# mLSTM cell and multiplicative FFN on one core: input rows loaded once, ScalarE copies, and y through DRAM as whole rows

## The chip, the core and the metric

The kernel runs on one core of one Trainium2 chip. Such a core has TensorE (PE in the profile; its weight loads are listed apart as PEld), VectorE (DVE), ScalarE (ACT), GpSimd (POOL) and SyncE (SP), which issues most of the DMAs. Each engine works through its own instructions in program order; engines wait for each other only through semaphores. A DMA that an engine issues waits in that engine's queue of instructions like any other instruction, and what stands behind it waits too.

The metric is the device time of one execution in microseconds (us), lower is better.

## The reference, cut to what matters

```python
# mLSTM cell; q, k, v, o_gate: (4, 8, 768, 40), gates: (4, 8, 768)
for t in range(S):
    m_new = np.maximum(f_gate[:, :, t] + m, i_gate[:, :, t])
    f_stab = np.exp(f_gate[:, :, t] + m - m_new)
    i_stab = np.exp(i_gate[:, :, t] - m_new)
    C = f_stab * C + i_stab * np.einsum('bhd,bhe->bhde', vt, kt)
    n = f_stab * n + i_stab * kt
    h_tilde = np.einsum('bhde,bhe->bhd', C, qt)
    denom = np.maximum(np.abs(np.einsum('bhd,bhd->bh', n, qt)), 1.0)
    y[:, :, t] = sigmoid(o_gate[:, :, t]) * h_tilde / denom
# FFN on x = y as (3072, 320)
out = ((x @ w1) * (x @ w2)) @ w3 @ w_out        # 320 -> 1024 -> 1024 -> 320
```

## The kernel before, in words

**Units and steps.** The sequence is cut into 24 units: unit n is 128 tokens of one batch entry (`c, b = divmod(n, 4)`) with all 8 heads. The main loop (L820) runs over 32 steps s. Step s computes the scores and the state update of unit s and the outputs of unit s-1, and around them the FFN of earlier units. PE's instructions are chained in program order by `in_order` (L84). The other engines follow the order in which the loop emits their instructions.

**Inside a step** (`quarter_work`, L338). PE multiplies the masked weights with v (`ph`, L363: the own outputs, from the unit's own tokens), the queries with the state (`pi`, L366), keys with queries (`ss`, L389) and keys with weighted values (`pc`, L394). `ph` and `pi` lie in the PSUM tile cell[1], `ss` and `pc` in cell[0]. DVE then makes the outputs of unit s-1 (`outputs`, L419): h = pi x gate (L423), plus `ph` in four quarters of 64x164 (L430), then the denominator from the 41st column of h, which is the normalizer's product because v carries a column of ones (L534): absolute value (L438), maximum with 1 and times 2 (L440), reciprocal (L441), (tanh+1) x reciprocal into the gate's tile (L443), times h into y (L445). Between these stand the masked scores (L397) and the two state additions (L404, L414); POOL multiplies the state by its decay (L335) between the two additions.

**Weights of a unit.** ACT makes the exponentials (L303, eight instructions), POOL cuts the triangle out of them (`masks`, L308) and weights v (L330).

**Turned queries and keys.** Up to unit 9 PE transposes k and q and ACT copies them out (`turn`, L320 to L325). From unit 10 on the loads `load_turned` (L141) bring rows of four tokens (160 elements), and two DVE transposes of 32x32 blocks (L317) give kT and qT. One head of 40 elements needs two blocks, of 32 and of 8 columns, so every row is loaded twice, the second time into 32 other partitions and 32 columns further left: 8 DMAs of 80 KB for a unit. `load_turned(s + 2)` is emitted at the end of step s (L975), into one of two buffers (halves of `gates` and `q_all`).

**From y to the FFN.** The FFN wants x with channels in partitions. Up to unit 14 (NY = 15, L126) PE transposes y in three 128x128 blocks (`x_trans`, L478) and ACT copies them out (L486). These run at the start of step n+3, at L849. POOL first copies the last 64 columns of y once more (`twice`, L475), for a pair of 64-row matmuls. From unit 15 on y goes to DRAM and back: `send(s - 2)` at the start of step s writes 32-column pieces by four DMAs (L451), `get_back(s - 2)` reads them by four DMAs into the one buffer `yb` (L462), and `x_turn(s - 2)` transposes them on DVE after the step's outputs (L926).

**FFN.** Units are taken in groups of four. Groups 0 to 2 go through `up` (L618): 24 blocks, of which steps 14 and 15 do the last four, for units 10 and 11. Groups 3 to 5 go through `up_by_seven` (L668), which forms products by a seven-product scheme. It needs sums of the weights, made by POOL in steps 16 and 17 (`weight_sums`, L651, eight additions of 128x512), and sums of the tokens of a group, made by DVE (`token_sums`, L661), for group 3 in step 17, behind the turned y of unit 15 and kT and qT of unit 18. In steps 19 to 24 its first products (p15) go into cell[1], from where ACT copies them out (L702, L704), and then the output matmuls of earlier groups (`ffn_out`, L733) write to the same banks of cell[1]. Before that, in steps 16 to 18, PE has little FFN work other than `ffn_out`.

**SP's queue** in a step, in order: send (from step 17), U rows (L159), k, v and o_gate of unit s+2 (L139, L153), get_back, at the step's end load_turned, and the weights still to come (L184, up to step 12).

Of the kernel before, what the change touches and what calls it, by code (L numbers as in the profile page):

```python
# [8 lines left out]
FP = mybir.dt.float32  # L9
U32 = mybir.dt.uint32  # L10
AF = mybir.ActivationFunctionType
OP = mybir.AluOpType
# [4 lines left out]
def kernel(  # L17
# [41 lines left out]
    KF = DM // P  # L59
    REM = DM - KF * P  # L60
# [7 lines left out]
    sb = ctx.enter_context(tc.tile_pool(name="sb", bufs=2))  # L68
    dram = ctx.enter_context(tc.tile_pool(name="dram", bufs=1, space=bass.MemoryType.DRAM))
# [39 lines left out]

    NB, NBQ, NBV = 4, 3, 5  # L110
    N_DVE = N_U = 10
    N_DIAG = 2
# [4 lines left out]
    vbuf = [v_all[:, i * H * D1:(i + 1) * H * D1].rearrange("p (h d) -> p h d", d=D1) for i in range(NBV)]  # L117
# [5 lines left out]
    decay = const.tile([P, B * NP, NT], FP, name="decay")  # L123
    UT = const.tile([P, 2, 3, BH], FP, name="UT")
    U_d = dram.tile([NT, BH, L], FP, name="U_d")
    NY = 15  # L126
    KC = KF + 1
    y_d = [dram.tile([P, 4, KC, 32], FP, name=f"y_d{n}") if n >= NY else None for n in range(NU)]

    o_t, u_t = {}, {}  # L130

# [9 lines left out]
    def load_turned(n):  # L141
        c, b = divmod(n, B)
        for dst, src in zip(turned_in[n % 2], (k, q)):
            for hip in range(2):
                of = src[b].rearrange("(p two) s d -> two p s d", two=2)[hip, :, c * P:(c + 1) * P, :]
                for j in range(2):
                    p0, c0 = hip * DP + j * 32, (1 - j) * 32
                    nc.sync.dma_start(out=dst[p0:p0 + 32, c0:c0 + NP * RAW].rearrange("r (p e) -> r p e", p=NP),  # L148
                                      in_=of.rearrange("p (r f) d -> r p (f d)", f=4))

    def load_o(n):
        o_t[n] = io.tile([P, H, D], FP, name="o_in", tag="o_in", bufs=5)
# [80 lines left out]
    def scale_next(early=False):  # L233
        scaled.append(pend.pop(0))
        scale(scaled[-1][1], early)
# [31 lines left out]
    qT_t, kT_t, vw_t, before_t, y_t, x_t = {}, {}, {}, {}, {}, {}  # L267
# [43 lines left out]
    def turn(n):  # L311


        if n >= N_DVE:
            for src, dst, name in zip(turned_in[n % 2], (kT_t, qT_t), ("kT", "qT")):
                dst[n] = sb.tile([128, NP, P], FP, name=name, tag=name)
                done = nc.vector.transpose(out=dst[n].rearrange("i p (r f) -> i p f r", f=4),  # L317
                                           in_=src[:, 32:TB].rearrange("i (p f d) -> i p f d", p=NP, f=4)[:, :, :, 0:32])
# [100 lines left out]
    def outputs(n, pi, ph):  # L419
        c, b = divmod(n, B)  # L420
        hs = slice(b * H, (b + 1) * H)
        h = sb.tile([P, H, D1], FP, name="h", tag="h")
        nc.vector.tensor_tensor(out=h.rearrange("p (n two) d -> p two n d", two=2), in0=pi,  # L423
                                in1=gT[:, c, hs].rearrange("p (n two) -> p two n", two=2).unsqueeze(3)
                                .to_broadcast([P, 2, NP, D1]), op=OP.mult)
        if n < N_DIAG:
            nc.vector.tensor_tensor(out=h, in0=ph, in1=h, op=OP.add)
        for x, e in quarters if n >= N_DIAG else ():
            part = h[halves[x], 0:H // 2] if x == e else h[halves[x], H // 2:H]
            nc.vector.tensor_tensor(out=part, in0=ph[x][halves[e]], in1=part, op=OP.add)  # L430

        den = sb.tile([P, H, 1], FP, name="den", tag="den")

        def steps():
            V = nc.vector
            yield V.tensor_scalar(out=den.bitcast(U32), in0=h[:, :, D:D1].bitcast(U32), scalar1=0x7FFFFFFF, scalar2=None,  # L438
                            op0=OP.bitwise_and)
            yield V.tensor_scalar(out=den, in0=den, scalar1=1.0, scalar2=2.0, op0=OP.max, op1=OP.mult)  # L440
            yield V.reciprocal(out=den, in_=den)  # L441
            e = o_t.pop(n)
            nc.vector.scalar_tensor_tensor(out=e, in0=e, scalar=1.0, in1=den.to_broadcast([P, H, D]), op0=OP.add, op1=OP.mult)  # L443
            y_t[n] = sb.tile([P, DM + REM], FP, name="y", tag="y")
            yield nc.vector.tensor_tensor(out=y_t[n][:, 0:DM].rearrange("p (h d) -> p h d", d=D), in0=h[:, :, 0:D],  # L445
                                           in1=e, op=OP.mult)

        done = steps()
        return lambda: next(done)

    def send(n):  # L451


        y = y_t.pop(n)
        for cc in range(KF):
            nc.sync.dma_start(out=y_d[n][:, :, cc, :], in_=y[:, cc * P:(cc + 1) * P].rearrange("t (i c) -> t i c", c=32))
        for i in range(0, 4, 2):
            nc.sync.dma_start(out=y_d[n][:, i:i + 2, KF, :], in_=y[:, KF * P:DM].rearrange("t (i c) -> t i c", c=32))

    back_t = {}  # L460

    def get_back(n):  # L462
        back_t[n] = sb.tile([P, 4, KC, 32], FP, name="yb", tag="yb", bufs=1)
        for i in range(4):
            nc.sync.dma_start(out=back_t[n][32 * i:32 * (i + 1)].rearrange("r m k c -> r m (k c)"),
                              in_=y_d[n][:, i].rearrange("(m r) k c -> r m (k c)", r=32))

    def x_turn(n):
        gr, j = divmod(n, GT)
        if j == 0:  # L470
            x_t[gr] = ffn.tile([128, KC, TG], FP, name="xT", tag="xT")
        nc.vector.transpose(out=x_t[gr][:, :, j * P:(j + 1) * P].rearrange("c k (m r) -> c k m r", r=32),
                            in_=back_t.pop(n).rearrange("r m k c -> r k m c"))

    def twice(n):  # L475
        nc.gpsimd.tensor_copy(out=y_t[n][:, DM:DM + REM], in_=y_t[n][:, KF * P:DM])
# [13 lines left out]
    TC = GC * L  # L490
    RG = GR * BH
    RAW = 4 * D
    TB = 32 + NP * RAW
    gates = const.tile([P, 2 * TB], FP, name="gates")
    f_sb, a, F, U, on = (gates[0:RG, i * TC:(i + 1) * TC] for i in range(5))

    turned_in = [[mem[:, i * TB:(i + 1) * TB] for i in range(2)] for mem in (gates, q_all)]
    w, g = f_sb, on
# [32 lines left out]
        if i < NBQ:  # L531
            nc.gpsimd.memset(qbuf[i][:, :, D:DP], 0.0)
    for i in range(NBV):
        nc.gpsimd.memset(vbuf[i][:, :, D:D1], 1.0)  # L534
    for t in state:
        nc.gpsimd.memset(t[0], 0.0)
    nc.gpsimd.memset(gates[:, 5 * TC:2 * TB], 0.0)
    nc.gpsimd.memset(gates[RG:P, NP * RAW:TB], 0.0)
# [279 lines left out]
    turned, converted, fetched = 0, 2, 5  # L818

    for s in range(len(n_up)):  # L820
        if NY <= s - 2 < NU:
            send(s - 2)
        if N_U <= s + 3 < NU:
            load_u(s + 3)
        if s < 3:
# [16 lines left out]
        if s < NU:  # L842
            if s >= B:
                decayed(state[s % B][1], state[s % B][0], s, 0)
        if s == 2 or N_DVE < s < NY + 2:
            twice(s - 2)
        if NY <= s - 2 < NU:
            get_back(s - 2)
        while s >= N_DVE and turned < min(s - 2, NY):  # L849
# [68 lines left out]
        with tc.issue_after(gated.ins) if gated else nullcontext():  # L918
            if seven:
                seven[3]()  # L920
            for _ in range({NU: 1, NU + 1: 3}.get(s, 0)):
                next(wsums)
            if s == NU + 1:
                ab_sums(*summed.pop(0))
            if NY <= s - 2 < NU:
                x_turn(s - 2)  # L926
            for n in () if s == 1 else (s + 2,) if s < B else (s + 2, s + 3) if s == B else (s + 3,):
                if n < N_U:
                    rows_of_u(n)
            if N_DVE <= s + 1 < NU:  # L930
                gated = turn(s + 1)
            if s - 2 in range(4 * GT - 1, NU, GT):
                token_sums((s - 2) // GT)
            if s < len(n_up) - 2 and n_out[s + 1] and s > NU + 2:
                ab_sums(*summed.pop(0))
# [76 lines left out]
```

## Time and profile before

| | |
|---|---|
| runs, us | 424.92, 426.45, 426.75; median 426.45 |
| span of the profiled execution, first to last instruction | 425.8 us |
| time of the profiled execution beyond its span | not listed; the median of the runs is 0.65 us above the span |
| busy in the span, PE / PEld / DVE / ACT / POOL | 414.1 / 335.3 / 313.5 / 150.1 / 154.3 us |
| mean granted TensorE clock | 0.996 |
| DMA | 51.15 MB, 120 GB/s in the mean |

The busy time of an engine is the time in which it shows an instruction at work. The chain of waits follows the work back from the last instruction. The timeline lists the instructions of each engine with start, duration and, in square brackets, how long the engine stood idle before it and what ended that. In this document "step 16" means s = 16, and times are us from the start of the span.

### The profile page before, as it was taken

How to read it: one execution, taken by the hardware profiler on the slowest of the kernel's cores; microseconds unless marked ns; L12 is line 12 of the kernel's file. 1: busy time of each engine (PE TensorE's matmuls, PEld its weight loads, DVE VectorE, ACT ScalarE, POOL GpSimd, SP SyncE). 2: the span in 40 equal slices, each digit the busy share in tenths (PEclk: the TensorE clock that was granted, in tenths of full speed). 3: DMA queues.
4: the chain of work that ended last, by engine and by line, in shares of the span. 5: the costliest groups of instructions: out<-in, count | busy, mean ns of one | idle time of the engine just before them, and what ended most of it. 6: DMA issues, size and time to landing. Idle time of an engine off the chain costs nothing.

```text
span 425.8 us, 13079 instructions
## 1 busy us (share of the span) xinstructions
PE 414.1 (97%) x5353; PEld 335.3 (79%) x5353; DVE 313.5 (74%) x635; ACT 150.1 (35%) x404; POOL 154.3 (36%) x211
## 2 busy tenths in 40 slices
PE   7989989999999999999999999999999999999996
PEld 4768878888688788787777778788778879888896
DVE  6676986888949779778736966596868699575971
ACT  4766865567723623630433313032311110210000
POOL 4421342233303303303307751546453587542100
PEclk9989999999999999999999999999999999999999
DMA  8999998598977776985425675756421120000001
GB/s 186 204 173 245 214 144 140 134 193 180 215 183 154 166 182 135 181 164 105 89 80 130 153 141 121 142 133 117 87 44 36 35 39 2 31 2 31 2 32 62
DMA packets 135211, 51.15 MB, mean 120 GB/s; under 512 B 109360, under 2 KB 126960, under 8 KB 135152
## 3 DMA queue, kind: packets, MB, share of 16 engines
q1 hardware_dynamic: 131552, 46.29, 53.9%
q10 hardware_dynamic: 3600, 4.03, 2.7%
q8 instruction: 42, 0.69, 0.7%
q14 instruction: 17, 0.14, 0.1%
HBM read 44.50 MB, written 5.80 MB: 118 GB/s over the span
## 4 chain that ended last, share of the span: by engine, by line
PE 53%; issue 20%; DVE 7%; POOL 7%; SPq 7%; DMA 5%; ACT 1%; POOLq 0%; DVEq 0%
PE cell L92 17%; PE pa L92 12%; PE o L92 8%; PE pb L92 8%; PE p L92 3%; POOL pw L308 3%; SPq L184 3%; DVE w3T L666 2%; PE pt L95 1%; POOL vw L330 1%; SPq L148 1%; DMA raw<-in_moe_w_dram 1%; PE fill L92 1%; POOL raw L659 1%; POOL state L335 1%
## 5 line engine op out<-in xcount | busy, mean ns | idle before, releaser
L335 POOL TENSOR_TENSOR state<-state,decay 128x164 f32<-128x164 f32 x40 | 20.0, 500 | 154.8 <-DVE state L404 129.0
L92 PE MATMUL pa<-xT,w 128*128 128x256 f32 x240 | 60.4, 382 | 0.0
L92 PEld LDWEIGHTS pa<-xT,w 128*128 128x128 f32 x240 | 44.4, 190 | 6.8 <-DVE h L430 0.4
L303 ACT ACTIVATE pw<-pw,aT 128x64 f32<-128x64 f32 x184 | 46.4, 339 | 3.2 <-ACT o_sb L741 1.9
L92 PE MATMUL pb<-xT,w 128*128 128x256 f32 x192 | 45.4, 379 | 0.0
L729 POOL TENSOR_TENSOR ab<-ab,a_sb 128x512 f32<-128x512 f32 x22 | 29.4, 1356 | 32.2 <-DVE ab L684 32.2
L92 PEld LDWEIGHTS pb<-xT,w 128*128 128x128 f32 x192 | 36.4, 190 | 5.0
L711 POOL TENSOR_TENSOR wo<-wo 128x512 f32<-128x512 f32 x22 | 27.4, 1268 | 29.8 <-DVE wo L686 29.8
L92 PE MATMUL pa<-xT,wr 64*64 64x256 f32 x384 | 37.0, 386 | 0.5 <-DVE wr L200 0.5
L92 PE MATMUL wp<-wo,w3T 128*128 128x320 f32 x128 | 35.9, 433 | 1.1 <-DVE ab L639 0.6
L308 POOL TENSOR_SCALAR_AFFINE_SELECT pw<-pw 64x512 f32<-64x512 f32 x48 | 35.8, 746 | 3.0 <-ACT pw L303 1.2
L92 PE MATMUL pb<-xT,wr 64*64 64x256 f32 x384 | 36.4, 380 | 0.0
L92 PE MATMUL cell<-w3o,ab 128*128 128x320 f32 x128 | 35.4, 432 | 0.0
L638 ACT ACTIVATE a_sb<-pa 128x512 f32<-128x512 f32 x24 | 14.3, 598 | 59.0 <-PE pb L92 59.0
L639 DVE TENSOR_TENSOR ab<-pb,a_sb 128x512 f32<-128x512 f32 x24 | 16.4, 688 | 23.2 <-ACT a_sb L638 22.8
L92 PEld LDWEIGHTS wp<-wo,w3T 128*128 128x128 f32 x128 | 23.8, 190 | 10.5 <-DVE ab L639 0.8
L92 PEld LDWEIGHTS cell<-w3o,ab 128*128 128x128 f32 x128 | 24.3, 190 | 9.5
L92 PEld LDWEIGHTS pa<-xT,wr 64*64 64x64 f32 x384 | 18.9, 132 | 15.4 <-issue 8.8
L686 DVE SCALAR_TENSOR_TENSOR a_sb<-pa,wo 128x512 f32<-128x512 f32 x12 | 8.3, 689 | 29.8 <-PE pa L92 29.8
L430 DVE TENSOR_TENSOR h<-cell,h 64x164 f32<-64x164 f32 x88 | 28.6, 326 | 1.6
L92 PE MATMUL po<-w3o,ab 128*128 128x320 f32 x96 | 26.4, 433 | 0.0
L92 PEld LDWEIGHTS po<-w3o,ab 128*128 128x128 f32 x96 | 18.1, 190 | 7.3
(180 smaller groups left out, 846.4 us busy)
## 6 DMA issues: line engine op xcount, KB each, us to landing
raw<-in_moe_w_dram SPq DMA_DIRECT2D x64, 128.0 KB, 3.4
kbuf<-in_k_dram SPq DMA_DIRECT2D x24, 160.0 KB, 4.5
v_all<-in_v_dram SPq DMA_DIRECT2D x24, 160.0 KB, 4.9
o_in<-in_o_gate_dram SPq DMA_DIRECT2D x24, 160.0 KB, 4.8
pw<-U_d SPq DMA_DIRECT2D x28, 128.0 KB, 3.5
raw<-in_moe_w_dram SPq DMA_DIRECT2D x5, 512.0 KB, 6.7
raw<-in_moe_w_out_dram SPq DMA_DIRECT2D x8, 320.0 KB, 4.1
gates<-in_k_dram SPq DMA_DIRECT2D x28, 80.0 KB, 2.5
```

What stands on the lines that cost most here:

```text
L92: in_order(nc.tensor.matmul(out, lhsT=lhsT, rhs=rhs, start=start, stop=stop))
L184: nc.sync.dma_start(out=dst, in_=src)
L303: nc.scalar.activation(out=pw[:, h, :], in_=src[:, h, :], func=AF.Exp, bias=aT[:, c, b * H + h:b * H + h + 1])
L308: nc.gpsimd.affine_select(out=pw[r], in_=pw[r], compare_op=OP.is_ge, fill=0.0, base=0, pattern=[[0, H], [1, L]], channel_multiplier=-1)
L335: nc.gpsimd.tensor_tensor(out=new, in0=old, op=OP.mult, in1=decay[:, b * NP:(b + 1) * NP, 2 * c + x:2 * c + x + 1] .to_broadcast([P, NP, D1]))
L430: nc.vector.tensor_tensor(out=part, in0=ph[x][halves[e]], in1=part, op=OP.add)
L638: nc.scalar.mul(out=a_sb, in_=pa, mul=UP ** -2)
L639: nc.vector.tensor_tensor(out=ab_t[gr][j][:, fs[0]:fs[-1] + 1, t0:t0 + a_sb.shape[-1]], in0=pb, in1=a_sb, op=OP.mult)
L666: nc.vector.tensor_tensor(out=dst, in0=p, in1=q, op=OP.subtract)
L686: nc.vector.scalar_tensor_tensor(out=out, in0=p, scalar=UP ** -2, in1=q, op0=OP.mult, op1=OP.add)
L711: aside_by.tensor_tensor(out=kept[j][:, 1:4:2], in0=kept[j][:, 1:3], in1=kept[j][:, 3:4].to_broadcast([128, 2, TH]), op=OP.add)
L729: aside_by.tensor_tensor(out=t[:, f:FO:FH, :], in0=t[:, f:FO:FH, :], in1=a, op=OP.mult)
```

## The change

- `load_turned` loads every row of four tokens once (4 DMAs of 80 KB in place of 8). A new function `shift` lets ACT copy the last 8 columns of each token into the 32 other partitions: four copies of 32x(16x8) for a unit, emitted in step n-1 ahead of the exponentials. POOL clears 32 partitions of `gates` for it in step 4.
- NY goes from 15 to 10: y of units 10 to 14 goes through DRAM too, and their PE transposes and ACT copies go away. `y_d` holds whole rows of 384 columns, written by one DMA and read by four of 384 pieces of 32 columns. So POOL's `twice` now runs for all units. `twice(s - 1)` and `send(s - 1)` stand at the end of step s, ahead of `load_turned`; `get_back` stays.
- From unit 10 (N_OWN) ACT copies the four quarters of `ph` out of PSUM into h, DVE writes pi x gate into the tile that later holds y, and adds both by one instruction of 128x328.
- The column of ones holds 2. The denominator is min(|1/x|, 0.5): reciprocal, one small instruction for the absolute value, the minimum and the product with h, and (tanh+1) times that: four instructions in place of five.

In the two programs' instruction lists, POOL's `twice` of units 15 and 16 stands behind the four additions of `weight_sums` of steps 16 and 17. ACT's `shift` stands behind the copies of `ph` and ahead of the exponentials. The first of the four copies of `ph` waits for DVE.

```diff
-                for j in range(2):
-                    p0, c0 = hip * DP + j * 32, (1 - j) * 32
-                    nc.sync.dma_start(out=dst[p0:p0 + 32, c0:c0 + NP * RAW]...)
+                nc.sync.dma_start(out=dst[hip * DP:hip * DP + 32, 32:TB].rearrange("r (p e) -> r p e", p=NP),
+                                  in_=of.rearrange("p (r f) d -> r p (f d)", f=4))
+    def shift(n):
+        for mem in turned_in[n % 2]:
+            e = mem[:, 32:TB].rearrange("r (g d) -> r g d", d=D)
+            for p0 in (0, DP):
+                nc.scalar.copy(out=e[p0 + 32:p0 + 64, :, 0:D - 32], in_=e[p0:p0 + 32, :, 32:D])
...
-    NY = 15
+    NY = 10
-    y_d = [dram.tile([P, 4, KC, 32], FP, ...) if n >= NY else None for n in range(NU)]
+    y_d = [dram.tile([P, KC * P], FP, ...) if n >= NY else None for n in range(NU)]
...
+        y = y_t[n] = sb.tile([P, DM + REM], FP, name="y", tag="y")
+        before = y[:, 0:H * D1].rearrange("p (h d) -> p h d", d=D1) if n >= N_OWN else h
...
+        if n >= N_OWN:
+            for x, e in quarters:
+                nc.scalar.copy(out=h[halves[x], 0:H // 2] if x == e else h[halves[x], H // 2:H], in_=ph[x][halves[e]])
+            nc.vector.tensor_tensor(out=h, in0=before, in1=h, op=OP.add)
...
+            yield V.reciprocal(out=den, in_=h[:, :, D:D1])
+            yield V.scalar_tensor_tensor(out=den, in0=den, scalar=-1.0, in1=den, op0=OP.mult, op1=OP.max)
+            v = h[:, :, 0:D]
+            yield V.scalar_tensor_tensor(out=v, in0=den.to_broadcast([P, H, D]), scalar=0.5, in1=v, op0=OP.min, op1=OP.mult)
+            yield V.scalar_tensor_tensor(out=y[:, 0:DM]..., in0=o_t.pop(n), scalar=1.0, in1=v, op0=OP.add, op1=OP.mult)
...
 def send(n):
+        nc.sync.dma_start(out=y_d[n], in_=y_t.pop(n))
 def get_back(n):
         for i in range(4):
+            nc.sync.dma_start(out=back_t[n][32 * i:32 * (i + 1)],
+                              in_=y_d[n].rearrange("(r m) (k i c) -> i r m k c", r=32, k=KC, i=4)[i])
...
-        nc.gpsimd.memset(vbuf[i][:, :, D:D1], 1.0)
+        nc.gpsimd.memset(vbuf[i][:, :, D:D1], 2.0)
...
-        if NY <= s - 2 < NU:
-            send(s - 2)
             if N_DVE <= s + 1 < NU:
+                shift(s + 1)
                 gated = turn(s + 1)
         if s in (16, 17):
             weight_sums(s - 16)
         if s == B:
+            nc.gpsimd.memset(gates[RG:P, 0:5 * TC], 0.0)
...
+        if NY <= s - 1 < NU:
+            twice(s - 1)
+            send(s - 1)
         if N_DVE <= s + 2 < NU:
             load_turned(s + 2)
```

More of the change, by code (lines that the diff above doesn't have):

```diff
@@ L111 @@
     N_DVE = N_U = 10
-    N_DIAG = 2
+    N_DIAG, N_OWN = 2, 10
     q_all = const.tile([P, NBQ * H * DP], FP, name="q_all")
@@ L125 @@
     U_d = dram.tile([NT, BH, L], FP, name="U_d")
-    NY = 15
+    NY = 10
     KC = KF + 1
-    y_d = [dram.tile([P, 4, KC, 32], FP, name=f"y_d{n}") if n >= NY else None for n in range(NU)]
+    y_d = [dram.tile([P, KC * P], FP, name=f"y_d{n}") if n >= NY else None for n in range(NU)]
     o_t, u_t = {}, {}
@@ L145, in load_turned @@
                 of = src[b].rearrange("(p two) s d -> two p s d", two=2)[hip, :, c * P:(c + 1) * P, :]
-                for j in range(2):
-                    p0, c0 = hip * DP + j * 32, (1 - j) * 32
-                    nc.sync.dma_start(out=dst[p0:p0 + 32, c0:c0 + NP * RAW].rearrange("r (p e) -> r p e", p=NP),
-                                      in_=of.rearrange("p (r f) d -> r p (f d)", f=4))
+                nc.sync.dma_start(out=dst[hip * DP:hip * DP + 32, 32:TB].rearrange("r (p e) -> r p e", p=NP),
[5 more added lines that the diff above has]
+                nc.scalar.copy(out=e[p0 + 32:p0 + 64, :, 0:D - 32], in_=e[p0:p0 + 32, :, 32:D])
     def load_o(n):
@@ L422, in outputs @@
         h = sb.tile([P, H, D1], FP, name="h", tag="h")
-        nc.vector.tensor_tensor(out=h.rearrange("p (n two) d -> p two n d", two=2), in0=pi,
+        y = y_t[n] = sb.tile([P, DM + REM], FP, name="y", tag="y")
+        before = y[:, 0:H * D1].rearrange("p (h d) -> p h d", d=D1) if n >= N_OWN else h
+        nc.vector.tensor_tensor(out=before.rearrange("p (n two) d -> p two n d", two=2), in0=pi,
                                 in1=gT[:, c, hs].rearrange("p (n two) -> p two n", two=2).unsqueeze(3)
@@ L427, in outputs @@
             nc.vector.tensor_tensor(out=h, in0=ph, in1=h, op=OP.add)
-        for x, e in quarters if n >= N_DIAG else ():
+        if n >= N_OWN:
+            for x, e in quarters:
+                nc.scalar.copy(out=h[halves[x], 0:H // 2] if x == e else h[halves[x], H // 2:H], in_=ph[x][halves[e]])
+            nc.vector.tensor_tensor(out=h, in0=before, in1=h, op=OP.add)
+        for x, e in quarters if N_DIAG <= n < N_OWN else ():
             part = h[halves[x], 0:H // 2] if x == e else h[halves[x], H // 2:H]
@@ L437, in steps @@
             V = nc.vector
[L438 to L446, printed above, removed]
+            yield V.reciprocal(out=den, in_=h[:, :, D:D1])
+            yield V.scalar_tensor_tensor(out=den, in0=den, scalar=-1.0, in1=den, op0=OP.mult, op1=OP.max)
+            v = h[:, :, 0:D]
+            yield V.scalar_tensor_tensor(out=v, in0=den.to_broadcast([P, H, D]), scalar=0.5, in1=v, op0=OP.min, op1=OP.mult)
+            yield V.scalar_tensor_tensor(out=y[:, 0:DM].rearrange("p (h d) -> p h d", d=D), in0=o_t.pop(n), scalar=1.0,
+                                         in1=v, op0=OP.add, op1=OP.mult)
         done = steps()
@@ L451, in send @@
     def send(n):
[L454 to L458, printed above, removed]
+        nc.sync.dma_start(out=y_d[n], in_=y_t.pop(n))
     back_t = {}
@@ L464, in get_back @@
         for i in range(4):
-            nc.sync.dma_start(out=back_t[n][32 * i:32 * (i + 1)].rearrange("r m k c -> r m (k c)"),
-                              in_=y_d[n][:, i].rearrange("(m r) k c -> r m (k c)", r=32))
+            nc.sync.dma_start(out=back_t[n][32 * i:32 * (i + 1)],
+                              in_=y_d[n].rearrange("(r m) (k i c) -> i r m k c", r=32, k=KC, i=4)[i])
     def x_turn(n):
@@ L471, in x_turn @@
             x_t[gr] = ffn.tile([128, KC, TG], FP, name="xT", tag="xT")
-        nc.vector.transpose(out=x_t[gr][:, :, j * P:(j + 1) * P].rearrange("c k (m r) -> c k m r", r=32),
+        nc.vector.transpose(out=x_t[gr][:, :, j * P:(j + 1) * P].rearrange("c k (r m) -> c k m r", r=32),
                             in_=back_t.pop(n).rearrange("r m k c -> r k m c"))
@@ L537 @@
     nc.gpsimd.memset(gates[:, 5 * TC:2 * TB], 0.0)
-    nc.gpsimd.memset(gates[RG:P, NP * RAW:TB], 0.0)
     nc.gpsimd.memset(pick, 0.0)
@@ L820 @@
     for s in range(len(n_up)):
-        if NY <= s - 2 < NU:
-            send(s - 2)
+        if s == 2 or N_DVE < s < NY + 2:
+            twice(s - 2)
         if N_U <= s + 3 < NU:
@@ L844 @@
                 decayed(state[s % B][1], state[s % B][0], s, 0)
-        if s == 2 or N_DVE < s < NY + 2:
-            twice(s - 2)
         if NY <= s - 2 < NU:
```

## The prediction

> **What bounds the kernel now.** I read the page's busy shares first, then its 40 slices, then the timeline of the steps that the change touches.
>
> ```profile
> span 425.8 us, 13079 instructions
> ...
> PE 414.1 (97%) x5353; PEld 335.3 (79%) x5353; DVE 313.5 (74%) x635; ACT 150.1 (35%) x404; POOL 154.3 (36%) x211
> ...
> PE   7989989999999999999999999999999999999996
> PEclk9989999999999999999999999999999999999999
> ```
>
> PE works 97% of the span at nearly the full clock. So two things alone move the end: PE instructions that come or go, and waits that the change puts in PE's way. Work saved on DVE, ACT, POOL or SP is worth nothing by itself; it counts only where PE waits for it, which it hardly does after the first 60 us.
>
> **Part 1, transposes of y (gain).** Five units (10 to 14) lose theirs.
>
> ```profile
> 174.22 0.55 PE L95 MATMUL px<-ident,y 128*128 128x128 f32 x3
> 174.61 4.47 PE L92 MATMUL wp<-wo,w3T 128*128 128x320 f32 x16
> 178.92 1.89 PE L92 MATMUL pa<-xT,w 128*128 128x256 f32 x8
> ```
>
> From the start of the three transposes to the next matmul is 174.61 - 174.22 = 0.39 us. Five units make 1.95 us. The last one stands in step 17, where I expect a wait (part 3) that swallows it, so I count four: **-1.56 us**. The ACT copy that goes with them (0.465 us, L486) runs beside PE.
>
> **Part 2, shorter outputs.** DVE's four quarter additions (L430, 4 x 0.326 = 1.34 us) become one of 128x328, which I take at 0.49 as L423; the denominator loses one instruction of some 0.2. ACT gets four copies of 64x164 out of PSUM. No such copy is in the trace; 128x96 takes 0.24 us, 128x192 0.32 us; I take 0.27, 1.1 us for four, ends 0.8 and 1.4. They start when DVE has written pi x gate. DVE's addition waits for them, so y is ready at most 0.5 us earlier. PE waits for DVE only at the start and twice by 0.4 us (at 242.8 and in the landing after 345): **-0.4 us** (0 to -0.8). Clearing 32 partitions on POOL in step 4 (some 1.1 us, estimated from a 128x192 memset of 0.26 us) lies in POOL's 129 us of waits for L404.
>
> The Trainium skill (PSUM — Partial Sum Buffer, "PSUM bank collisions raise a hardware error") forbids two engines in the same bank and quadrant at once, even to read. It speaks against letting ACT read `ph` while DVE reads `pi` from the same tile; the changed order makes ACT wait out DVE's 0.49 us, and without that wait each copy could start about 0.5 us sooner. No run shows what a collision would do; the sum stands without this.
>
> **Part 3, the y way and the turned rows (loss).** SP issues 56 loads fewer, but their order changes. `send(n)` now waits on SP for POOL's `twice(n)`, and `load_turned` stands behind `send`. That matters in steps 16 and 17, where POOL's `twice` is queued behind four additions. The next lines are those of POOL, SP, DVE, PE and ACT:
>
> ```profile
> 223.62 1.76 POOL L308 TENSOR_SCALAR_AFFINE_SELECT pw<-pw 64x512 f32<-64x512 f32 x2
> 225.47 1.28 POOL L659 TENSOR_TENSOR raw<-w 128x512 f32<-128x512 f32 x1
> ...
> 229.28 1.28 POOL L659 TENSOR_TENSOR raw<-w,raw 128x512 f32<-128x512 f32 x1
> ```
> ```profile
> 231.05 3.05 SPq L465 DMA_DIRECT2D yb<-y_d  x4
> 234.20 1.80 SPq L148 DMA_DIRECT2D q_all<-in_k_dram  x4
> ```
> ```profile
> 235.87 0.58 DVE L472 STREAM_TRANSPOSE xT<-yb 128x384 f32<-128x384 f32 x1
> 236.37 1.08 DVE L317 STREAM_TRANSPOSE kT<-gates 128x512 f32<-128x512 f32 x1
> 237.28 1.11 DVE L317 STREAM_TRANSPOSE qT<-gates 128x512 f32<-128x512 f32 x1
> ```
> ```profile
> 242.83 0.70 PE L92 MATMUL pa<-w3T,w 128*128 128x256 f32 x2 [0.41 <-DVE w3T L666]
> ...
> 248.55 8.78 PE L92 MATMUL cell<-w3o,ab 128*128 128x320 f32 x32
> ```
> ```profile
> 242.80 0.46 ACT L270 ACTIVATE o_in<-o_in 128x320 f32<-128x320 f32 x1
> 247.02 0.60 ACT L704 ACTIVATE wo<-cell 128x512 f32<-128x512 f32 x1 [3.77 <-PE cell L92]
> ```
>
> Before, ACT sat idle 3.77 us ahead of L704, and the turned rows of unit 18 were issued at 210.93, a step early. After the change, by the durations of these rows:
>
> 1. Step 16. The copies of `ph` follow L423 (ends 219.9) and take 1.1; `shift(17)` 4 copies. Their size, 32x128, is not in the trace; nearest are the exponentials of 128x64, one every 0.25 us, and a 128x96 copy, 0.24; ends 0.17 and 0.34, I take 0.25, so 1.0 us. The eight exponentials take 2.0: to 224.1. Masks 1.77: 225.9. Four additions 5.1: 231.0. `twice(15)`, 0.24: 231.3.
> 2. SP: the send 0.64, four turned loads of 0.45: issued by 233.8. The turned loads land 2.3 us after issue: 235.7.
> 3. ACT, step 17: `shift(18)` 1.0, exponentials 2.0: 238.7. POOL: masks 240.5, additions 5.2 to 245.7, `twice(16)` 246.0.
> 4. SP: send, turned loads of unit 19 by 248.5, landed 250.4.
> 5. ACT, step 18: `shift(19)` 1.0, exponentials 2.0, tanh (L270) 0.46. L704 follows in ACT's order and takes 0.60: 254.5. Only then may `ffn_out` overwrite the bank: at 254.6 in place of 248.55, **+6.1 us**.
>
> Each round holds one POOL block and one load, 14.7 us from `twice(15)` to `twice(16)`, while PE's step before was 10.7 us. Nothing else can hide it: PE goes in order, and steps 16 to 18 hold little FFN work.
>
> Inside these 6.1 us lie two earlier waits. U row, k, v and o of SP take 3.4 us after 233.8, so yb(15) is issued 237.2 to 239.9 and lands at about 241.7 (2.0 after issue). x_turn, kT and qT follow (0.57 + 2.05): 244.4, where PE wants them at 240.4. Then the token sums (0.42 to 1.49 each) let PE go on near 247.5 in place of 242.83. From there 4.2 us of products precede L704 as before: 251.7, still ahead of ACT's 253.9, so ACT is what ends last. Bounds: the short ends of the copies take off 1.2, and if `shift` works on k while q is still landing, 0.5 to 0.7 more in each round: +3.5. Copies at their long ends (1.0 in all) and landings 0.5 us longer in each round: +8.
>
> PE's idle time may lower the clock. In the windows of one microsecond PE is busy 0.04 at 22 to 23, and the granted clock is 0.71, 0.50, 0.50, 0.59 in the next four. That loses 0.29 + 0.50 + 0.50 + 0.41 = 1.7 us of full-speed work. Put on the 4.2 us of products ahead of L704 it makes 253.4, still ahead of ACT's 253.9. So I add nothing.
>
> The Trainium skill (TensorE: Matmul & The Clock Gate, "Part 1: The HAM clock gate") tells of a free-running window of about 3.4 us and half rate after an idle one. By that rule, as an estimate, a wait of 2 us costs nothing more or 1.7 us more, by where it falls in the window; the rows above show the half rate, and the sum would be 432.8 or 434.5.
>
> **Part 4, x of unit 11 (loss).** Unit 11 still goes through the `up` blocks of step 14, which start at 178.92, 178.53 without the transposes. Its y now goes by DRAM: yb(11) is issued between 174 and 177, behind k, v and o, among loads that landed up to 5.1 us after issue (174.42 to 179.5). I take landing at 180.0 and x_turn 0.57: 180.6, **+2.0 us** (0 if it lands by 178, 3.5 if at 181.5). The yb reads are now 1536 pieces of 128 bytes in place of 512 of 384; their only price row is 2.0 to 4.1 us from issue to landing.
>
> **Part 5, the seven-product steps 20 to 22.** There L704 ended about 0.2 us ahead of PE's need of the bank; ACT now does 2.1 us more a step, partly in idle time: **+0.3 us** (0 to 2).
>
> **Sum.** -1.56 - 0.4 + 2.0 + 6.1 + 0.3 = +6.4 us: span 425.8 + 6.4 = 432.2. The median of the runs stands 0.65 above the profiled span, so 432.8 us, 6.4 above the median of 426.45. With all terms at their good ends it is -1.56 - 0.8 + 0 + 3.5 + 0 = +1.1, 427.6; at their bad ends -1.56 + 0 + 3.5 + 8 + 2 = +11.9, 438.4.
>
> **Rivals.** About 0.5%, 2.1 us, is what a measurement here can tell from no change.
>
> - *Nothing waits, PE only loses its transposes.* -1.95 - 0.4: 424.1 us. It decides if yb(15) lands by 237.9 (2.6 ahead of 240.4) and unit 19's rows by 244.5 (3.5 us of ACT work ahead of 248). For it: DMA is light there (89 to 130 GB/s against 204 at the start), and 56 issues are gone. Against it: POOL's additions alone, 5.1 us twice, fix the earliest times. Chance 0.13.
> - *One wait is hidden.* Step 14 waits and the chain of step 16 does not (-1.96 + 2.0: 426.5), or yb(11) is in time and the chain stands at its short end (-1.96 + 3.5, with part 5 at most +0.5: 428.5). So 426.5 to 428.5. Chance 0.14.
> - *The chain as worked out*, 429 to 436, likeliest 432.8. Chance 0.57.
> - *More than that*: half clock after each wait (1.7 us, twice), ACT late in every seven-step (+2), landings at their long ends: 436 to 440. Chance 0.16.
>
> The range leaves out the first rival (0.13) and the last one's end above 438 (0.06): 426.0 to 438.0. Chances: faster by over 0.5% 0.13, within 0.5% 0.14 and slower 0.73.
>
> **What would show it.** Right: POOL's `twice(15)` ends near 231 and `twice(16)` near 246 (shifted with PE); SP's queue waits at the send; PE idles some 4 us ahead of the scores of step 18 and again ahead of `ffn_out`, released by ACT L704's line; a wait of some 2 us ahead of `up` at 178.5, released by DVE's transpose. Wrong: `twice(15)` done well ahead of the additions, PE busy through 240 to 255, or ACT's copies of 32 and 64 partitions much longer than 0.34 us, which would move the wait into every step from 10 on.

## The result, and the profile after

The changed kernel takes 445.15 us (median of 4 runs, 443.55 to 446.03) against 426.24 us before (4 runs): a ratio of 1.0444, 95% interval 1.0418 to 1.0471. It is 18.9 us slower; the prediction had 6.4. The measured time lies outside the predicted range of 426.0 to 438.0. One run of experiment 1, 444.84 us, is over 1.5% above the fastest of its kernel and counts as a slow execution; the medians leave it out.

Line numbers below are those of the changed kernel unless another is named: L437 copies of `ph` on ACT, L154 `shift`, L308 exponentials, L196 and L200 weight conversions, L490 ACT's copy of x, L480 `twice`, L662 weight sums, L462 send, L469 the reads of y (yb), L476 and L322 the DVE transposes, L705 and L707 ACT's copies of p15.

The page of the changed kernel:

```profile
span 443.4 us, 13084 instructions
...
PE 418.4 (94%) x5338; PEld 337.2 (76%) x5338; DVE 295.4 (67%) x574; ACT 179.4 (40%) x511; POOL 156.8 (35%) x220
...
PE   7898999999999899599999499999999999999997
PEclk9999999999999899799999889999999999999999
```

Three new dips stand in PE's row (slices 14, 17 and 23), each with a dip of PEclk in the same slice, and DVE's busy time fell by 18 us to no use. PE's busy time rose by 4 us though 15 transposes are gone: some of the same matmuls ran at a lower clock (the mean of the 128x256 products into `pa` rose from 382 to 399 ns). PE's timeline names the three waits and a small one that recurs:

```profile
148.22 2.89 PE L92 MATMUL pa<-xT,w 128*128 128x256 f32 x8 [1.90 <-ACT xT L490]
```
```profile
185.28 3.75 PE L92 MATMUL pa<-xT,w 128*128 128x256 f32 x8 [5.09 <-DVE xT L476]
```
```profile
254.57 1.13 PE L92 MATMUL cell<-qT,kT 40*64 40x64 f32 x32 [5.60 <-DVE qT L322]
```
```profile
301.48 0.81 PE L92 MATMUL cell<-w3o,ab 128*128 128x320 f32 x2 [0.38 <-ACT wo L705]
```

Where the time came from is read best from the starts of the scores on PE, one per step, in both timelines. The difference of the two intervals is what a step cost. An interval holds what stands behind the scores of one step and ahead of those of the next.

| stretch | before, us | after, us | difference |
|---|---|---|---|
| start to scores of step 11 | 142.03 | 139.63 | -2.40 |
| to scores of step 12 | 15.99 | 20.06 | +4.07 |
| to step 13 | 15.29 | 15.01 | -0.28 |
| to step 14 | 15.29 | 22.72 | +7.43 |
| to steps 15, 16, 17 | 41.52 | 40.68 | -0.84 |
| to step 18 | 10.68 | 16.47 | +5.79 |
| to step 19 | 19.13 | 20.22 | +1.09 |
| to steps 20, 21, 22, 23 and the end | 165.9 | 168.6 | +2.7 |

The sum is +17.6, the difference of the spans. The medians differ by 18.9, as the runs of the changed kernel stand 1.75 us above their spans, while the median of before stands 0.65 us above the span of its profiled execution.

### The profile page after: what moved, and what is told of

Read it like the earlier page. It is cut to its first block, busy times and chain, and to the rows that moved or that the text cites. A ratio compares the mean times of both kernels' runs of the same rounds, so it can differ in the third digit from the quotient of the medians.

```text
span 443.4 us, 13084 instructions
## 1 busy us (share of the span) xinstructions
PE 418.4 (94%) x5338; PEld 337.2 (76%) x5338; DVE 295.4 (67%) x574; ACT 179.4 (40%) x511; POOL 156.8 (35%) x220
## 4 chain that ended last, share of the span: by engine, by line
PE 49%; SPq 12%; issue 10%; DVE 10%; DMA 8%; ACT 7%; POOL 3%; DVEq 0%; POOLq 0%; ACTq 0%
PE cell L92 12%; PE pa L92 12%; PE o L92 8%; PE pb L92 7%; SPq L139 4%; PE po L92 4%; SPq L189 4%; PE p L92 3%; PE wp L92 3%; ACT pw L308 2%; DMA raw<-in_moe_w_dram 2%; DMA yb<-y_d 1%; ACT h L437 1%; DVE ab L687 1%; SPq L158 1%
## 5 line engine op out<-in xcount | busy, mean ns | idle before, releaser
L340 POOL TENSOR_TENSOR state<-state,decay 128x164 f32<-128x164 f32 x40 | 22.6, 564 | 165.4 <-DVE state L409 146.3
L92 PE MATMUL pa<-xT,w 128*128 128x256 f32 x240 | 63.8, 399 | 7.0 <-DVE xT L476 5.1
L92 PEld LDWEIGHTS pa<-xT,w 128*128 128x128 f32 x240 | 46.0, 198 | 14.7 <-issue 5.6
L92 PE MATMUL pb<-xT,w 128*128 128x256 f32 x192 | 47.1, 389 | 1.1 <-DVE w L205 1.1
L308 ACT ACTIVATE pw<-pw,aT 128x64 f32<-128x64 f32 x184 | 46.4, 336 | 0.4
L92 PEld LDWEIGHTS pb<-xT,w 128*128 128x128 f32 x192 | 37.8, 197 | 7.1 <-DVE w L205 1.5
L313 POOL TENSOR_SCALAR_AFFINE_SELECT pw<-pw 64x512 f32<-64x512 f32 x48 | 32.0, 667 | 13.9 <-ACT pw L308 8.8
L437 ACT COPY h<-cell 64x164 f32<-64x164 f32 x56 | 16.2, 289 | 38.3 <-DVE y L430 37.8
```

Of the source, the lines that this page charges most:

```text
L92: in_order(nc.tensor.matmul(out, lhsT=lhsT, rhs=rhs, start=start, stop=stop))
L308: nc.scalar.activation(out=pw[:, h, :], in_=src[:, h, :], func=AF.Exp, bias=aT[:, c, b * H + h:b * H + h + 1])
L313: nc.gpsimd.affine_select(out=pw[r], in_=pw[r], compare_op=OP.is_ge, fill=0.0, base=0, pattern=[[0, H], [1, L]], channel_multiplier=-1)
L340: nc.gpsimd.tensor_tensor(out=new, in0=old, op=OP.mult, in1=decay[:, b * NP:(b + 1) * NP, 2 * c + x:2 * c + x + 1] .to_broadcast([P, NP, D1]))
L437: nc.scalar.copy(out=h[halves[x], 0:H // 2] if x == e else h[halves[x], H // 2:H], in_=ph[x][halves[e]])
```

## The experiments

Twelve kernels were run. "Before" is always the kernel before in the same comparison, 425.4 to 425.8 us. The changed kernel itself was timed only in the result, where before took 426.24; so a difference to its 445.15 carries 0.4 to 0.9 us of that shift, and the intervals between scores are the safer measure.

**1. Reads of y of unit 11 issued earlier.** `get_back(11)` stands behind `load_turned` of step 12:

```diff
             load_turned(s + 2)
+        if s - 1 == 11:
+            get_back(11)
-        if NY <= s - 2 < NU:
+        if NY <= s - 2 < NU and s - 2 != 11:
             get_back(s - 2)
```

> The changed kernel, but the reads of y of unit 11 (yb) are issued at the end of step 12, ahead of the eight weight loads and of k, v, o of step 13. Theory (SP's queue makes step 14 wait): yb(11) is issued near 170 in place of 179.0 and landed by 175; the transpose on DVE then stands behind that step's outputs (y of unit 12 ends at 180.45) and takes 0.86, so PE still waits some 1.2 us in place of 5.09: 3.9 us less, 441.3 us; if the clock also stays up, up to 6.3 less, 438.9. Rival (the 128-byte pieces are slow to land, wherever they are issued): the wait stays near 5 us, 444 to 446 us.

438.93 us, 6.2 less than the changed kernel. The loads were issued from 167.32 and the wait fell as expected, without a drop of the clock:

```profile
179.13 1.97 PE L92 MATMUL pa<-xT,w 128*128 128x256 f32 x8 [1.19 <-DVE xT L476]
```

The interval to step 14 is 16.44 us, 6.28 less than in the changed kernel. The place in SP's queue made the wait, not the small pieces, which are the same here.

**2. ACT copies own outputs only from unit 12.** `N_OWN = 12`.

> The changed kernel, but ACT copies own outputs only from unit 12, so in steps 11 and 12 DVE adds them as before. Theory (ACT's copy of x of unit 9 at 147.71 is late because the copies of ph, which begin only at 140.72 after DVE, and shift stand ahead of it): that copy ends near 145.7, the 1.90 us wait of step 12 and the half clock behind it go, 4.1 us less: 441.1 us. Rival (shift alone, or the weights' conversions, make it late): the wait stays over 1 us and the time within 1 us of 445.2.

441.27 us, 3.9 less. ACT's timeline of step 11 without the copies:

```profile
139.42 1.26 ACT L154 COPY gates<-gates 32x128 f32<-32x128 f32 x4
140.70 2.02 ACT L308 ACTIVATE pw<-pw,aT 128x64 f32<-128x64 f32 x8
...
145.27 0.46 ACT L490 COPY xT<-px 128x384 f32<-128x384 f32 x1
```

In the changed kernel the same copy started at 147.71. PE's wait is gone (interval to step 12: 16.16 us), while the one of step 14 stays at 4.70 us. The theory holds: `shift` alone, still ahead of that copy, does not make it late.

**3. Weight sums last on POOL.**

```diff
-        if s in (16, 17):
-            weight_sums(s - 16)
...
             twice(s - 1)
             send(s - 1)
+        if s in (16, 17):
+            weight_sums(s - 16)
```

> The changed kernel, but the weight sums of steps 16 and 17 stand on POOL behind twice and SP's send and turned loads. Theory (twice(15) and twice(16) queued behind POOL's four additions make the chain of step 18 late): twice(15) ends near 234.5 in place of 239.5, yb(15) lands near 246.7 in place of 251.8, the 5.60 us wait for kT and qT of unit 18 falls to 0 to 1 us and the half clock after it goes: 5.3 to 6.9 us less, 438.3 to 439.9. Rival (yb(15)'s place behind U, k, v and o on SP sets it): the wait stays over 3 us, 443 to 445.

439.97 us, 5.2 less. `twice(15)` started at 233.65 in place of 239.27, and the wait fell from 5.60 to 1.49, where 0 to 1 was expected; the half clock came all the same:

```profile
249.86 0.69 PE L92 MATMUL cell<-qT,kT 40*64 40x64 f32 x32 [1.49 <-DVE qT L322]
```

What is left is the rival's part: yb(15) still stood behind U, k, v and o on SP and was issued from 241.62. So POOL's order made most of the wait, SP's order a smaller part. In experiment 8, which moves both, the wait is gone.

**4. Idle matmuls in the wait of step 14.** `if s == 14: warm(5)` ahead of the up blocks.

> The changed kernel with five idle matmuls of 128x512 (some 0.95 us each) on PE ahead of the up blocks of step 14, inside its 5.09 us wait. They compute nothing that is used. Theory (the wait costs a second time through the granted clock, 0.50 from 184 to 190): the clock holds, 2 to 2.4 us less, 442.8 us. Rival (the clock's drop costs nothing, as other engines set the pace there): 445 us, or more by what of the filler does not fit.

443.24 us, but this kernel's runs spread over 442.07 to 446.46, so the median says little; the profile says it. The windows of one microsecond show the busy time of PE, PEld, DVE, ACT and POOL, then the clock, DMA share and GB/s; first the changed kernel, then this one:

```profile
188.00:189.00 1.00, 1.00 (x4) 0.82 (x3) 1.00 (x2) 0.00 (x0) 0.00 (x0) 0.50 1.39 215
```
```profile
188.00:189.00 1.00, 1.00 (x6) 0.90 (x5) 1.00 (x3) 0.00 (x0) 0.00 (x0) 1.00 0.46 140
```

With the filler the clock stays at 1.00 and the interval to step 14 is 19.43 us in place of 22.72, 3.3 less. Not all of that is the clock's, as the reads also landed earlier in this run:

```profile
186.29 0.87 DVE L476 STREAM_TRANSPOSE xT<-yb 128x384 f32<-128x384 f32 x1 [2.96 <-DMA yb<-y_d]
```

The transpose of y of unit 11 ends 9.6 us after the scores of step 13 (187.16 against 177.57); in the changed kernel it was 10.4 (185.13 against 174.70). That is 0.8 of the 3.3; the other 2.4 is what the windows of the changed kernel give for the clock.

**5. Units 10 and 11 transposed on PE again.** `NY = 12`.

> The changed kernel, but y goes through DRAM only from unit 12, so units 10 and 11 are transposed on PE and copied out by ACT as before. The yb wait of step 14 cannot come. Theory (ACT's queue, made longer by the copies of ph and shift, is a cause by itself): ACT's copy of x of unit 11 ends near 183.3 where PE wants it at 180.3, so PE waits 2.6 to 3.0 us in place of 5.09, and pays 0.28 twice for the transposes: 442 to 443.5 us. Rival (only the way through DRAM is to blame at step 14): no wait there, 7.4 less 0.6, 438 to 439 us.

443.57 us, just above the theory's upper end. The wait of step 14 has another releaser now:

```profile
183.40 1.78 PE L92 MATMUL pa<-xT,w 128*128 128x256 f32 x7 [2.88 <-ACT xT L490]
```

So two parts of the change each make step 14 late. The interval to step 14 fell from 22.72 to 18.44 us, for the wait is 2.2 us shorter and the clock did not drop, but the total by 1.6 only: the chain of step 18 took 0.8 us more, and the half clock behind it lasted 10.3 us in place of 6.8, which cost 0.9 more in the next interval.

**6. The kernel before with the shorter denominator alone.**

```diff
-            yield V.tensor_scalar(out=den.bitcast(U32), ...)
-            yield V.tensor_scalar(out=den, in0=den, scalar1=1.0, scalar2=2.0, op0=OP.max, op1=OP.mult)
-            yield V.reciprocal(out=den, in_=den)
...
+            yield V.reciprocal(out=den, in_=h[:, :, D:D1])
+            yield V.scalar_tensor_tensor(out=den, in0=den, scalar=-1.0, in1=den, op0=OP.mult, op1=OP.max)
...
-        nc.gpsimd.memset(vbuf[i][:, :, D:D1], 1.0)
+        nc.gpsimd.memset(vbuf[i][:, :, D:D1], 2.0)
```

> The kernel before with the shorter denominator alone (column of ones 2, four instructions). Theory (the shorter DVE chain is what makes the changed kernel 2.4 us earlier up to step 11, by the 1.19 us wait at 22.96 and the half clock after it): 1.5 to 2.4 less than before, 423 to 424 us where before is at 425.4. Rival (the gain of the first steps comes from the fewer loads or from chance in the clock): within 0.5 us of before.

425.15 us against 425.84, ratio 0.9985 (0.9959 to 1.0011): no difference that can be measured. The theory about the 2.4 us of the first steps is not borne out.

**7. Own outputs by ACT only for units 10 to 17.**

> The changed kernel, but ACT copies own outputs only for units 10 to 17; from unit 18 DVE adds them as before. Theory (these copies, begun after DVE, push ACT's L707 and L705 behind PE in the seven-product steps, 0.65 us a step): PE's 0.38 us waits for L705 go, 2.0 to 2.6 less, 442.6 to 443.2. Rival (shift's 1.25 us is enough to be late): half or less of it goes, 444 to 445.

440.93 us, 4.2 less and more than expected. The timeline gives 2.7 to these steps (none of PE's waits for L705 is left); the profiled execution also gained 1.7 in step 12, where the clock did not drop, which is no effect of this edit. ACT now comes early:

```profile
296.05 0.60 ACT L707 ACTIVATE wo<-cell 128x512 f32<-128x512 f32 x1 [2.64 <-PE cell L92]
```

**8. Four orders changed together.** Own outputs by ACT only for units 12 to 17; the sums last; all reads of y at the end of the step that sent it; `x_turn(11)` ahead of step 13's outputs.

> The changed kernel with four orders changed: own outputs by ACT only for units 12 to 17, weight sums behind twice and send, the reads of y issued at the end of the step that sent it (ahead of weights, U, k, v, o), and the transpose of unit 11 ahead of step 13's outputs on DVE. Theory (the loss is the four waits and the clock behind them, 4.1 + 7.4 + 6.9 + 2.6 = 21 us, and they are independent): 424 us, 1 to 1.5 below before. Rival (some of it is contention or a wait that moves elsewhere): 427 us or more.

425.14 us, 0.9984 of before (0.9955 to 1.0012). All of the loss is back; whether the 0.7 below before is a gain, as the theory had it, is within the noise. The profiled span is 422.9, and of the waits one for the token sums is left, which was 0.41 before:

```profile
239.21 0.70 PE L92 MATMUL pa<-w3T,w 128*128 128x256 f32 x2 [0.57 <-DVE w3T L669]
```

**9 to 11. One part of the change at a time, put on the kernel before.** In these kernels L491 is ACT's copy of x, and L473 and L317 are the DVE transposes. First the own outputs from unit 10:

> The kernel before with one part of the change: ACT copies the four quarters of ph from unit 10. Theory (the copies begin only after DVE's product and hold up the exponentials, the weights' conversions and the copy of x behind them): by before's rows the copy of x of unit 9 ends 0.7 to 1.0 us after PE wants it in step 12 and that of unit 11 1.7 us after in step 14: 2.4 to 2.7 us more, and 1.7 us more for each wait that drops the clock: 428.2 to 431.5 where before is 425.8; the seven-product steps nearly on time. Rival (ACT has room, 35% busy): within 0.5 us of before.

430.31 us, ratio 1.0108 (1.0091 to 1.0124). The waits are at the two places named:

```profile
146.92 1.35 PE L92 MATMUL pa<-xT,w 128*128 128x256 f32 x5 [1.40 <-ACT xT L491]
```
```profile
179.40 1.78 PE L92 MATMUL pa<-xT,w 128*128 128x256 f32 x7 [1.64 <-ACT xT L491]
```

Then the rows loaded once:

> The kernel before with one part of the change: turned rows loaded once and shifted by ACT. Theory (1.25 us of shift start at once, as their data are there, and fit into ACT's slack but for 0.4 us in step 14): 425.8 to 426.5 where before is 425.8. Rival (56 loads fewer relieve SP and the DMA and are worth something): 425.3 or less.

427.42 us, ratio 1.0045 (1.0015 to 1.0075), 1 us over what was expected. The profile shows the wait of step 14 (0.50 us) and one of 0.57 for token sums; of a gain by the fewer loads nothing shows. The rest of the 1.9 us does not show in the profiled execution (span 424.1) and stays open.

Then y through DRAM:

> The kernel before with one part of the change: y from unit 10 through DRAM as rows, sent at the end of the step after POOL's twice, ahead of load_turned, which still issues eight loads. Theory (the order of POOL and SP makes the waits of steps 14 and 18): 7.4 and 6.9 us as in the changed kernel, each some 1.8 longer by the four more issues ahead of get_back, less 1.4 for the transposes: 438 to 444 us. Rival (the waits need ACT's shift and copies as well): under 433 us.

443.07 us, ratio 1.0414 (1.0384 to 1.0445). Both waits come, and are 1.6 and 1.7 us longer than in the changed kernel, with four more issues ahead of the reads:

```profile
184.67 3.75 PE L92 MATMUL pa<-xT,w 128*128 128x256 f32 x8 [6.67 <-DVE xT L473]
```
```profile
255.03 1.14 PE L92 MATMUL cell<-qT,kT 40*64 40x64 f32 x32 [7.27 <-DVE qT L317]
```

The parts cost 4.8, 1.9 and 17.5 us, together 5.3 more than the 18.9 of the whole. Two things make up most of that: the two waits just shown are 3.3 us longer than in the whole, and ACT's lateness in step 14 (1.9 us in the interval of the first of these kernels) is hidden in the whole, where PE waits longer for yb.

**12. The version of experiment 8 without any own output on ACT.** `N_OWN = 18` there.

> The version with the four orders changed, and no own output copied by ACT at all (DVE adds all of them as before). Theory (DVE's time is not on the path, so the copies bring nothing): 425.1 within 0.7 us, the same as that version. Rival (the shorter DVE chain of units 12 to 17 is worth something): 426 us or more.

423.68 us against 425.54: ratio 0.9956 (0.9934 to 0.9979), a little faster than before and 1.5 us under the 425.14 of experiment 8. Neither theory nor rival had that. The two versions were timed in different comparisons and their intervals overlap, so the 1.5 is not shown. The profiles give a place for 1.0 of it: the interval from step 18 to 19 is 18.96 us in place of 19.94, as the wait for the token sums shown under experiment 8 is gone. There, DVE's addition had waited 1.26 us for ACT's copies.

## Why the prediction was wrong, point by point

The direction was right, and the chain of steps 16 to 18 was found. In spans the prediction had +6.4 and +17.6 us came. Two steps of it failed most. It put the effect of ACT's longer queue on step 12 at nothing, where it cost 4.07 us. And it took the wait for x of unit 11 in step 14 as 2.0 us with no loss by the clock, where it was 5.09 us and with the clock 7.43. Part 5 (2.4 short), part 3 (0.8) and part 1 (0.4) make up most of the rest; the first row of the table, -2.40, goes the other way. A further 1.1 lies between span and median: the prediction took 0.65 us, the changed kernel's runs have 1.75.

**A term was missing: step 12 (+4.07 us).** The prediction looked at ACT's copy of x only where it goes away ("runs beside PE") and at ACT's longer queue only in steps 16 to 22. But PE still transposes unit 9, ACT copies it, and the up blocks of step 12 need it at once. Before, that copy ended 1.5 us ahead of PE (146.82 against 148.34):

```profile
146.35 0.47 ACT L486 COPY xT<-px 128x384 f32<-128x384 f32 x1
```
```profile
148.34 1.89 PE L92 MATMUL pa<-xT,w 128*128 128x256 f32 x8
```

ACT's timeline of step 11 in the changed kernel:

```profile
140.72 1.19 ACT L437 COPY h<-cell 64x164 f32<-64x164 f32 x4 [1.16 <-DVE y L430]
141.94 1.25 ACT L154 COPY gates<-gates 32x128 f32<-32x128 f32 x4
143.22 2.02 ACT L308 ACTIVATE pw<-pw,aT 128x64 f32<-128x64 f32 x8
...
147.71 0.45 ACT L490 COPY xT<-px 128x384 f32<-128x384 f32 x1
```

The durations were sized well (1.1 and 1.0 predicted, 1.19 and 1.25 measured). What was not put to account is that everything ACT does in a step moves behind them, and that ACT first waits 1.16 us for DVE. Experiments 2 and 9 show it from both sides.

**Part 4, x of unit 11: predicted +2.0, measured +7.43.** The mechanism was right, the size not. The issue of yb(11) was taken from before's queue as 174 to 177, some 176 to 178.5 with the shift of 1.4 us of that step. SP's timeline shows why it was later; first before, where the last line is the slot that the reads were to take, then the changed kernel:

```profile
167.00 3.89 SPq L184 DMA_DIRECT2D raw<-in_moe_w_dram  x8
...
173.40 0.98 SPq L153 DMA_DIRECT2D o_in<-in_o_gate_dram  x1
174.42 3.20 SPq L148 DMA_DIRECT2D q_all<-in_k_dram  x4
```

```profile
167.12 0.35 SPq L462 DMA_DIRECT2D y_d<-y  x1
...
169.49 4.62 SPq L189 DMA_DIRECT2D raw<-in_moe_w_dram  x8
...
176.65 2.35 SPq L158 DMA_DIRECT2D o_in<-in_o_gate_dram  x1
179.03 3.03 SPq L469 DMA_DIRECT2D yb<-y_d  x4
```

Eight weight loads stand behind `send`, which waits for POOL's `twice` (ended 167.1): they begin 1.1 us later than before, measured from the scores of step 13, take 0.7 more, and the issue of o takes 1.4 more. So the reads begin 3.2 us later than that queue had it, and the wait is 3.1 us longer than the 2.0. The rest of the error, 2.4 us, is the clock, next. Landing was not the cause: 2.2 us after the last issue, where 3.0 were assumed. Experiment 1 undoes it.

**The clock: predicted "I add nothing", measured in three places.** Behind the waits of 1.90, 5.09 and 5.60 us the granted clock was 0.50 for a while (in the two long ones the drop came during the wait): by the windows, full-speed work of 1.7 us (steps 11 to 12), 2.4 us (step 14) and 1.9 us (step 18) was lost. The prediction considered the clock only where ACT would be the last to be ready anyway. Experiment 4 shows the price. A wait of 1.90 us dropped the clock in the changed kernel, one of 1.89 us at the same place in experiment 1 did not. The Trainium skill (TensorE: Matmul & The Clock Gate, "Part 1: The HAM clock gate") calls the window in which the activity is watched free-running and puts the half rate after an idle window of about 3.4 us. That two like waits differ would fit a free-running window, though no run shows the window itself; that waits under 2 us, much shorter than the window, dropped the clock at all does not follow from that rule, and here the measurement decides. The prediction's estimate by it, nothing or 1.7 us for a wait of 2 us, went beyond the rule, but both are what the runs show.

**Part 3, the chain of steps 16 to 18: predicted +6.1, measured 5.79 + 1.09 = 6.9.** With the scores of step 16 8.26 us later than before, the working can be followed instant by instant:

| | predicted + 8.26 | measured |
|---|---|---|
| `twice(15)` ended | 239.6 | 239.5 |
| turned rows of 18 issued by | 242.1 | 242.25 |
| yb(15) issued | 245.5 to 248.2 | 246.6 to 249.8 |
| landed | 250.0 | 251.83 |
| kT and qT of unit 18 done | 252.7 | 254.5 |
| `twice(16)` ended | 254.3 | 253.3 |

The POOL lines behind it are these; the additions between the first line and `twice` are the queue that was named:

```profile
234.25 1.28 POOL L662 TENSOR_TENSOR raw<-w 128x512 f32<-128x512 f32 x1
...
239.27 0.24 POOL L480 COPY y<-y 128x64 f32<-128x64 f32 x1
```

The chain up to `twice(16)` was right within 2 us at every instant, and the +6.1 came near; but that is partly luck, for which link ended last was wrong. PE waited for kT and qT (5.60 us, predicted 4.0), and the lower clock stretched the products behind; ACT's L707, which was to be the last, waited 0.42 us for PE. The sum also left out L702 (L705 after the change), the second of ACT's two copies, which in the rows of before ends 0.5 us after L704. Experiment 3 shows that POOL's order is the main cause.

**Part 1, transposes: predicted -1.56, measured -1.12.** Each of the four counted steps without transposes is 0.28 us shorter (15.01 in place of 15.29), not 0.39.

**Part 2, shorter outputs: predicted -0.4, not shown.** The first steps of the changed kernel are 2.4 us earlier, but so they are (2.46 us at step 11) in experiment 9, which changes nothing ahead of unit 10. The start of step 11 is no measure of the change: in the five profiles of kernels that are the same up to there (the changed kernel, experiments 1, 3, 4 and 7) it lies between 138.9 and 144.2 us. In the profile of before a wait of 1.19 us at 22.96 was followed by a half clock, in experiment 9 a wait of 1.13 us at the same place was not; but the clock is not all of it, as in experiment 6 it did not drop and step 11 still began at 141.91. The profiled execution of before seems to have been a long one: in later comparisons the runs of before stand 2.0 us above their spans, which puts a span of 425.8 at 427.8, above all four runs of the result. Experiment 6 finds nothing for the denominator. ACT's copies did not shorten DVE's chain either. From pi x gate to the finished y DVE took 5.46 us before (unit 15), 5.13 in the changed kernel (unit 12), and 4.78 in experiment 12 (unit 16), where DVE adds `ph` itself: the gain is the denominator's, and the copies took half of it back.

**Part 5, the seven-product steps: predicted +0.3, measured +2.7.** The four intervals from the scores of step 19 to those of step 23 are 0.65 us longer each; in the last three of them PE shows a wait of 0.38 us for L705. The prediction compared ACT's added work with its idle time, but ACT's work of a step now begins after DVE's product. In step 20 the first ACT lines are, before and after:

```profile
277.49 2.02 ACT L303 ACTIVATE pw<-pw,aT 128x64 f32<-128x64 f32 x8 [0.42 <-DMA kbuf<-in_k_dram]
```
```profile
295.61 1.19 ACT L437 COPY h<-cell 64x164 f32<-64x164 f32 x4 [3.04 <-DVE y L430]
```

The exponentials began 0.9 us ahead of the scores (278.38); now the copies begin 1.7 us after them (293.88), and the exponentials later still. Experiment 7 takes it away.

**The rivals.** The one with more of the same (436 to 440) had the clock and ACT's lateness in the later steps, and was still too short, since it lacked step 12 and the late reads of unit 11.

**Three readings of before.** They carry little, but the rows say otherwise. Ahead of PE's need of the bank (285.44 in step 20), L704 ended 0.9 us and the copy L702 behind it 0.4 us, not 0.2. After the first 60 us PE's waits for DVE are 0.58 us at 108.35, 0.41 at 242.83 and 0.22 at 356.12, not two of 0.4. And the DMA was not as light as 89 to 130 GB/s: windows of 2 us between 231 and 241 show 130 to 230.

## What to carry to other kernels

An engine that is 35% busy has no slack to spend in general: look, in each step, at the one instruction on it that the bound engine needs next, and at what is put ahead of that in its queue. When a transfer gets a new wait, follow it along the issuing queue past everything that stands behind it, weights for later steps too. And where the matmul engine was saturated, price a new wait with the clock behind it: here each of the three long waits came with 1.7 to 2.4 us of lost work.

## What the runs showed of the hardware

The clock behind a wait is not a function of the wait's length alone. Waits of PE that came with a drop: 1.19 (before), 1.48 (experiment 4, at 59.2 us), 1.49 and 2.00 (experiment 3), 1.90 (the changed kernel). Waits that did not: 1.49 (before, at 59.1 us), 1.19 and 1.89 (experiment 1), 1.64 (experiment 9), 1.98 (experiment 4), 2.88 (experiment 5). All from 4.65 us on did, unless filled with matmuls. The half clock came in stretches of about 3.4 us (after the waits of 1.19 to 2.00), 6.8 (after those of 4.65 to 5.60, 6.10 and 6.67) or 10.3 (after 6.00, 6.36 and 7.27). A stretch of 3.4 us takes 1.7 us of full-speed work, about as much as the short wait itself.

The DVE transpose of a unit's x took 0.86 to 0.93 us from the new yb layout, against 0.57 before, for the same 128x384 elements: only the order of the output columns and the reads' pieces differ. ACT's copies took 0.29 us (64x164, out of PSUM) and 0.30 us (32x128 in groups of 8 columns), between the 0.24 and 0.32 of 128x96 and 128x192: a half or a quarter of the partitions saved nothing.

SP's issue of o, one DMA, took 0.98 us in step 13 of before, and 2.35 and 2.58 us in two steps of the changed kernel. What held it there is not settled.
